# Layer norm of the next block, one row tile per chunk of a gated unit, in place of half a tile per chunk

## The chip, the cores and the metric

The kernel runs on one core of one Trainium2 chip. The metric is the device time of one execution in microseconds (us). Times before are the median of nine executions; one execution was also taken by the hardware profiler, and all durations and positions below come from that one.

The engines go by their short names: PE is TensorE (PEld its weight loads), DVE VectorE, ACT ScalarE, POOL GpSimd, SP the sync engine, which here only issues DMAs.

## The reference

```python
x = A_x                                   # 1 x 2048 x 640, bf16
xn = (x - mean(x)) / sqrt(var(x) + 1e-5)  # layer norm over the last axis

# A: attention, 32 heads of 192, over the last 512 of 2048 cached keys, no mask
q = (xn @ wq) per head                    # wq: 640 x 6144
p = softmax(q @ k.T * 192 ** -0.5)
s = (p @ v, heads side by side) @ wo      # wo: 6144 x 640

# B: gated unit, then a down projection
h = sigmoid(xn @ w_gate) * (xn @ w_up)    # 640 x 1536 each
g = silu(h @ w_down)                      # 1536 x 640
out = x + s * g
```

## The kernel before

The 2048 rows are 16 row tiles of 128 rows (`t`), four of them (`TQ`) to a block of 512 rows (`b`, `NB` = 4). The kernel first makes the normalized rows, transposed (`xnT`), and from them part B (`gate`), block by block, until about 177 us. The rest of the time is attention, eight groups of four heads over four blocks. The order of the instructions on each engine is written out by hand: the scheduler is in manual mode, so each engine runs its instructions in the order in which the program text issues them, and only semaphores and buffers make them wait.

**Gated unit.** `gated(b, f, ...)` (L219) makes one chunk of 128 of the 1536 columns for one block: five matmuls with `wg_sb` and five with `wu_sb` into the two halves of a PSUM bank pair (L227), the sigmoid on ACT (`sig`, L230), then an optional call `between()`, then the product on DVE (`hT`, L233). There are twelve chunks (`NF`) to a block. Four bank pairs take turns (`k`), so that chunk f + 4 needs the bank that the product of chunk f has read. What `between()` issues on DVE stands ahead of that product in DVE's order.

**Down projection.** `down(b, q, k)` (L236) makes `gate` for one row tile: 24 matmuls (L239), a sigmoid (L242), a product (L243).

**Layer norm of a row tile.** It has these parts:
- `stats_half(t, 0)` and `stats_half(t, 1)`: one `bn_stats` on DVE each, of half a row (`st`, L185)
- `stats_end(t)`: `bn_aggr` on DVE (`mv`, L190), then variance plus eps on DVE (`rstd`, L196), and its power of -0.5 on POOL (`rstd`, L197)
- `normal(t)`: subtract and multiply on DVE (`xn`, L203); it waits for POOL
- `turn_dma(t)`: one transposing DMA on SP's queue, from `xn` into `xnT` (L218). Matmuls of that block wait for its landing.

Block 0 has a path of its own at the start. The tiles of blocks 1, 2 and 3 are normalized during the gated unit of the block ahead: `norm_piece(b, i)` (L245) returns the i-th of eight half steps of block b, and the main loop hands it to `gated` as `between`. An even i is the statistics of a tile, an odd i its normalization and transpose. For block 1 they stand in chunks 4 to 11 of block 0, for blocks 2 and 3 in chunks 2 to 9 of the block ahead:

```python
gated(0, f, 0, TB, k, norm_piece(1, f - 4))          # f = 4 to 11
...
gated(b, f, 0, TB, k, norm_piece(b + 1, f - 2) if b + 1 < NB and f < 10 else None)
```

The order around it is: chunks 4 to 11 of block 0; then for b = 1, 2, 3: chunks 0 and 1 of block b, the four down projections of block b - 1, chunks 2 to 11 of block b. So the first matmul of a block's chunk 0 follows the last of chunk 11 of the block ahead, and needs the last row tile of its own block to be transposed.

Other work that the steps touch:
- `load_x(3 * TQ, TQ)` (L149): the rows of block 3, one DMA of 640 KB on SP's queue, behind the transposes of block 1. It takes the buffer that block 1's rows leave.
- `load_group(0)` (L97 to L112): after block 2's last chunk in the text, the first attention group's loads on POOL's queue (query weights `wq_sb` of 960 KB, keys `k_st` of 768 KB, four loads of values `vbuf` of 192 KB) and four copies of keys on POOL (`k_perm`). On POOL they follow directly on the power of row tile 15.
- `turn_keys(0)` (L128): transposing DMAs of the keys on SP, after block 3's last chunk in the text.

Of the kernel before, what the change touches and what calls it, by code (L numbers as in the profile page):

```python
# [15 lines left out]
def kernel(  # L16
# [28 lines left out]
    TB = 512  # L45
    NB = S // TB
    TQ = TB // P
# [45 lines left out]
    def load_group(g):  # L93

        d = grp.setdefault(g, {})
        d["wq"] = load2.tile([P, NCD, GW], BF16, name="wq_sb")
        nc.gpsimd.dma_start(d["wq"][:], wq_r[:, :, g * GW:(g + 1) * GW])  # L97
        kst = load1.tile([P, 4, KC, DH], BF16, name="k_st")
        kv = slice(Sk - W, Sk)
        nc.gpsimd.dma_start(  # L100
            kst[:].rearrange("p h j d -> p h (j d)"),
            A_k_cache[0, 4 * g:4 * g + 4, kv, :].rearrange("h (p j) d -> p h (j d)", j=KC),
        )
        d["v"] = vbuf[g % 2]
        for h in range(4):
            nc.gpsimd.dma_start(  # L106
                d["v"][:, h, :, 0:DH],
                A_v_cache[0, 4 * g + h, kv, :].rearrange("(p j) d -> p j d", j=KC),
            )
        kp = load1.tile([P, 2, KC, DJ, P], BF16, name="k_perm")  # L110
        for h in range(4):
            nc.gpsimd.tensor_copy(  # L112
                kp[:, h // 2, :, :, (h % 2) * H2:(h % 2) * H2 + H2],
                kst[:, h, :, :].rearrange("p c (i j) -> p c j i", j=DJ),
            )
        d["kp"] = kp
# [6 lines left out]
    def turn_keys(g):  # L123
        d = grp[g]
        d["kT"] = load2.tile([P, 2, DJ, W], BF16, name="kT")
        for pr in range(2):
            for c in range(KC):
                nc.sync.dma_start_transpose(  # L128
                    d["kT"][:, pr, :, c * P:(c + 1) * P],
                    d["kp"][:, pr, c, :, :].rearrange("p j i -> p (j i)"),  # L130
                )


    with ExitStack() as bctx:
# [11 lines left out]
        def load_x(t, n):  # L146

            x = xpool.tile([P, n, D], BF16, name=f"x_sb{n}", bufs=1 if n == 2 else 2)
            nc.sync.dma_start(x[:], xf[t * P:(t + n) * P, :].rearrange("(q p) d -> p q d", p=P))  # L149
            for i in range(n):  # L150
                xt[t + i] = x[:, i, :]
# [30 lines left out]
        def stats_half(t, i):  # L182
            if i == 0:
                ln[t] = bwork.tile([P, 2, nc.vector.BN_STATS_DIM], F32, name="st")
            nc.vector.bn_stats(ln[t][:, i, :], xt[t][:, i * (D // 2):(i + 1) * (D // 2)])  # L185

        def stats_end(t):
            mv = bwork.tile([P, nc.vector.BN_AGGR_DIM], F32, name="mv")
            rstd = bwork.tile([P, 1], F32, name="rstd")
            nc.vector.bn_aggr(mv[:], ln[t][:])  # L190
            if t == 0:
                nc.scalar.activation(rstd[:], mv[:, 1:2], AF.Sqrt, bias=eps_t[:], scale=1.0)
                nc.scalar.activation(junk[:], eps_t[:], AF.Sigmoid)
                nc.vector.reciprocal(rstd[:], rstd[:])
            else:
                nc.vector.tensor_scalar(rstd[:], mv[:, 1:2], eps, None, op0=ALU.add)  # L196
                nc.gpsimd.tensor_tensor(rstd[:], rstd[:], mhalf[:], ALU.pow)  # L197
            ln[t] = mv, rstd

        def normal(t):  # L200
            mv, rstd = ln[t]
            xn = xpool.tile([P, D], BF16, name="xn")
            nc.vector.tensor_scalar(xn[:], xt[t], mv[:, 0:1], rstd[:, 0:1],  # L203
                                    op0=ALU.subtract, op1=ALU.mult)
            ln[t] = xn
# [10 lines left out]
        def turn_dma(t):  # L216
            q = t % TQ
            nc.sync.dma_start_transpose(xnT[:, t // TQ, :, q * P:(q + 1) * P], ln[t][:])  # L218
# [3 lines left out]
        def gated(b, f, r0, r1, k, between=None):  # L222
            if b not in hT:
                hT[b] = hpool.tile([P, NF, TB], BF16, name="hT")
            for half, w in ((0, wg_sb), (1, wu_sb)):
                for c in range(NCD):
                    nc.tensor.matmul(bank[k][:, half, 0:r1 - r0], lhsT=w[:, c, f * P:(f + 1) * P],  # L227
                                     rhs=xnT[:, b, c, r0:r1], start=(c == 0), stop=(c == NCD - 1))
            sig = bwork.tile([P, TB], BF16, name="sig")
            nc.scalar.activation(sig[:, 0:r1 - r0], bank[k][:, 0, 0:r1 - r0], AF.Sigmoid)  # L230
            if between is not None:
                between()
            nc.vector.tensor_tensor(hT[b][:, f, r0:r1], bank[k][:, 1, 0:r1 - r0],  # L233
                                    sig[:, 0:r1 - r0], ALU.mult)

        def down(b, q, k):  # L236
            for f in range(NF):
                for d0, d1 in ((0, 512), (512, D)):
                    nc.tensor.matmul(wide(k)[:, d0:d1], lhsT=hT[b][:, f, q * P:(q + 1) * P],  # L239
                                     rhs=wd_sb[:, f, d0:d1], start=(f == 0), stop=(f == NF - 1))  # L240
            sg = bwork.tile([P, D], F32, name="sg", bufs=2)
            nc.scalar.activation(sg[:], wide(k)[:, 0:D], AF.Sigmoid)  # L242
            nc.vector.tensor_tensor(gate[:, b * TQ + q, :], wide(k)[:, 0:D], sg[:], ALU.mult)  # L243

        def norm_piece(b, i):  # L245

            t = b * TQ + i // 2

            def first():
                stats_half(t, 0)  # L250
                stats_half(t, 1)
                stats_end(t)

            def second():
                normal(t)
                turn_dma(t)

            return second if i % 2 else first


        dummy(19)
# [9 lines left out]
        k = 0  # L271
# [28 lines left out]
        k = 3  # L300
        for f in range(4, NF):
            gated(0, f, 0, TB, k, norm_piece(1, f - 4))
            k = (k + 1) % 4
        for b in range(1, NB):
            for f in range(2):
                gated(b, f, 0, TB, k)
                k = (k + 1) % 4
            for q in range(TQ):
                down(b - 1, q, k)
                k = (k + 1) % 4  # L310
            if b == 1:
                load_x(3 * TQ, TQ)
            for f in range(2, NF):
                gated(b, f, 0, TB, k, norm_piece(b + 1, f - 2) if b + 1 < NB and f < 10 else None)
                k = (k + 1) % 4
            if b == 2:
                load_group(0)
            if b == 3:
                turn_keys(0)
        for q in range(TQ):  # L320
            down(NB - 1, q, k)
            k = (k + 1) % 4
# [12 lines left out]
        for m in range(DJ):  # L335
# [3 lines left out]
            k = (k + 1) % 4  # L339
# [114 lines left out]
    for u in range(NU):  # L454
        g, b = u // NB, u % NB
# [67 lines left out]
```

The softmax here doesn't subtract the row's maximum and nothing guards it: scores larger than these inputs give would overflow.

## Time and profile before

| | |
|---|---|
| median of nine executions | 947.35 us (946.27 to 949.1) |
| the profiled execution, its own time | 946.27 us |
| its span in the profile | 944.5 us |
| PE busy | 919.6 us, 97% of the span |
| DVE busy | 471.0 us, 50% |
| ACT busy | 305.8 us, 32% |
| POOL busy | 132.6 us, 14% |
| mean granted PE clock | 0.995 of full |
| blocks 0 to 3 of part B, on the axis | to about 177 us |

The table's shares are over the whole span, and most of it is attention, which the change does not touch. A busy share says how long an engine had an instruction, not whether another waited for it. The chain that ended last is the view that follows, from the last instruction back, who released whom; the waits list how long an engine stood and which instruction released it, where the name given is the one that came last by the profile. The timeline shows instructions in order, each with the idle time ahead of it. All positions are in us from the span's start.

### The profile page before, as it was taken

The numbers are of one execution on the slowest core, as the hardware profiler recorded it, in microseconds if no ns is written. First come the engines' busy times: TensorE is split into PE (matmuls) and PEld (weight loads), VectorE is DVE, ScalarE is ACT, GpSimd is POOL, SyncE is SP. The second block draws the span as 40 slices with busy tenths as digits, with TensorE's granted clock in tenths as the row PEclk, the third lists the DMA queues.
The fourth block names the chain that finished last, engine by engine and source line by source line (L and its number), as shares of the span: only waits on it lengthen the run. The fifth ranks groups of instructions, "written<-read, shape, count | busy, mean of one in ns | idle before, by whom it ended". The sixth has DMA issues, their size and how long they took to land.

```text
span 944.5 us, 18100 instructions
## 1 busy us (share of the span) xinstructions
PE 919.6 (97%) x7962; PEld 546.7 (58%) x8042; DVE 471.0 (50%) x754; ACT 305.8 (32%) x342; POOL 132.6 (14%) x161
## 2 busy tenths in 40 slices
PE   7999979999999999999999999999999999999996
PEld 6455434566666666666666666666666666666664
DVE  5443513345555555555555555555555555555657
ACT  4222212253333333333333333333333333333340
POOL 1000210210020002000200020002000205555000
PEclk9999989999999999999999999999999999999999
DMA  9300240433523253425342433273325334422223
GB/s 312 79 15 15 61 109 1 142 86 49 129 68 76 49 129 67 76 47 130 68 73 52 130 68 76 47 131 68 76 46 131 69 68 80 86 62 62 63 62 90
DMA packets 156767, 76.69 MB, mean 81 GB/s; under 512 B 139024, under 2 KB 150032, under 8 KB 156688
## 3 DMA queue, kind: packets, MB, share of 16 engines
q1 hardware_dynamic: 146288, 42.86, 22.9%
q0 software_dynamic: 7936, 30.94, 11.9%
q10 hardware_dynamic: 2464, 1.74, 0.7%
q8 instruction: 63, 1.03, 0.5%
q14 instruction: 16, 0.13, 0.0%
HBM read 39.45 MB, written 2.62 MB: 45 GB/s over the span
## 4 chain that ended last, share of the span: by engine, by line
PE 95%; DMA 2%; DVE 2%; issue 1%; ACT 0%; SPq 0%; POOL 0%; DVEq 0%
PE bank L381 21%; PE bank L423 21%; PE bank L398 18%; PE bank L363 18%; PE bank L227 10%; PE bank L239 5%; DMA xnT<-xn 1%; PE bank L331 1%; DMA oT<-o_st 0%; DVE st L185 0%; DMA x_sb<-in_A_x_dram 0%; DVE row L445 0%; DVE row L429 0%; DVE o_sb L428 0%; DVE hT L233 0%
## 5 line engine op out<-in xcount | busy, mean ns | idle before, releaser
L367 ACT ACTIVATE E<-bank 128x1024 bf16<-128x1024 f32 x256 | 257.9, 1023 | 477.5 <-PE bank L363 465.6
L381 PE MATMUL bank<-xnT,wq_sb 64*128 64x512 bf16 x1860 | 231.3, 376 | 0.0
L423 PE MATMUL bank<-wo_sb,oT 128*128 128x512 bf16 (+1 forms) x1461 | 224.0, 296 | 5.3 <-DMA oT<-o_st 1.9
L363 PE MATMUL bank<-qT,kT 64*128 64x512 bf16 x1536 | 202.1, 376 | 0.2 <-DVE o_st L404 0.2
L398 PE MATMUL bank<-vbuf,E 128*128 128x193 bf16 x2048 | 191.0, 247 | 0.0
L398 PEld LDWEIGHTS <-E 128*128 128x128 bf16 x2048 | 167.8, 98 | 24.2 <-issue 13.6
L388 DVE CAST qT<-bank 128x1024 bf16<-128x1024 f32 x93 | 113.9, 1225 | 132.8 <-PE bank L381 132.8
L423 PEld LDWEIGHTS <-oT 128*128 128x128 bf16 x1524 | 120.3, 98 | 78.3 <-DMA oT<-o_st 2.6
L381 PEld LDWEIGHTS <-wq_sb 64*128 64x128 bf16 x1860 | 97.0, 100 | 104.8
L363 PEld LDWEIGHTS <-kT 64*128 64x128 bf16 x1536 | 73.1, 94 | 90.2 <-issue 8.9
L404 DVE TENSOR_TENSOR o_st<-bank,rden 128x768 bf16<-128x768 f32 x128 | 122.6, 957 | 4.6 <-DVE rden L403 0.2
L434 DVE TENSOR_TENSOR acc<-bank,acc 128x640 f32<-128x640 f32 x96 | 79.2, 825 | 43.7 <-PE bank L423 43.7
L227 PE MATMUL bank<-xnT,wg_sb 128*128 128x512 bf16 (+1 forms) x296 | 62.4, 340 | 9.9 <-DMA xnT<-xn 5.3
L233 DVE TENSOR_TENSOR hT<-bank,sig 128x512 bf16<-128x512 f32 (+1 forms) x60 | 35.0, 584 | 57.6 <-ACT sig L230 57.5
L227 PE MATMUL bank<-xnT,wu_sb 128*128 128x512 bf16 (+1 forms) x295 | 62.2, 339 | 0.3
L386 DVE COPY seen<-bank 128x2 f32<-128x2 f32 x93 | 14.8, 159 | 94.1 <-PE bank L381 94.0
L403 DVE RECIPROCAL rden<-bank 128x4 f32<-128x4 f32 x128 | 23.3, 182 | 71.3 <-PE bank L398 71.2
L230 ACT ACTIVATE sig<-bank 128x512 bf16<-128x512 f32 (+1 forms) x60 | 30.7, 512 | 85.3 <-PE bank L227 85.3
L239 PE MATMUL bank<-wd_sb,hT 128*128 128x128 bf16 (+1 forms) x376 | 52.4, 297 | 0.4
L106 POOL DMA_DIRECT2D vbuf<-in_A_v_cache_dram x32 | 23.9, 747 | 183.7 <-PE bank L398 183.7
L227 PEld LDWEIGHTS <-wg_sb 128*128 128x128 bf16 x300 | 26.7, 98 | 36.6 <-issue 12.2
L239 PEld LDWEIGHTS <-hT 128*128 128x128 bf16 x384 | 29.7, 98 | 23.1
(49 smaller groups left out, 263.2 us busy)
## 6 DMA issues: line engine op xcount, KB each, us to landing
wq_sb<-in_A_wq_dram POOLq DMA_DIRECT2D x8, 960.0 KB, 6.6
wo_sb<-in_A_wo_dram POOLq DMA_DIRECT2D x8, 960.0 KB, 7.1
k_st<-in_A_k_cache_dram POOLq DMA_DIRECT2D x8, 768.0 KB, 8.4
vbuf<-in_A_v_cache_dram POOLq DMA_DIRECT2D x32, 192.0 KB, 3.0
row<-in_A_x_dram POOLq DMA_DIRECT2D x16, 160.0 KB, 2.5
oT<-o_st SPq DMA_TRANSPOSE x132, 2.6
x_sb<-in_A_x_dram SPq DMA_DIRECT2D x3, 640.0 KB, 11.0
wd_sb<-in_B_w_down_dram SPq DMA_DIRECT2D x1, 1920.0 KB, 14.1
```

The source lines that it names most:

```text
L227: nc.tensor.matmul(bank[k][:, half, 0:r1 - r0], lhsT=w[:, c, f * P:(f + 1) * P], rhs=xnT[:, b, c, r0:r1], start=(c == 0), stop=(c == NCD - 1))
L230: nc.scalar.activation(sig[:, 0:r1 - r0], bank[k][:, 0, 0:r1 - r0], AF.Sigmoid)
L233: nc.vector.tensor_tensor(hT[b][:, f, r0:r1], bank[k][:, 1, 0:r1 - r0], sig[:, 0:r1 - r0], ALU.mult)
L239: nc.tensor.matmul(wide(k)[:, d0:d1], lhsT=hT[b][:, f, q * P:(q + 1) * P], rhs=wd_sb[:, f, d0:d1], start=(f == 0), stop=(f == NF - 1))
L363: nc.tensor.matmul(bank[k][:, i, :], lhsT=kT[r, pr, j, c * P:(c + 1) * P], rhs=q[r, pr * DJ + j, :], start=(j == 0), stop=(j == DJ - 1))
L367: nc.scalar.activation(E[u, pr][:, c, :, :], bank[k][:], AF.Exp, scale=scale_qk)
L381: nc.tensor.matmul(bank[k][:, half, :], lhsT=wq[r, c, col:col + DJ * (P - 1) + 1:DJ], rhs=xnT[r, b, c, :], start=(c == 0 and not second), ...
L388: nc.vector.tensor_copy(qT[u][:, 2 * m:2 * m + 2, :], bank[k][:])
L398: nc.tensor.matmul(o4[:, q, 0:DH + 1], lhsT=e[:, c, h % 2, q * P:(q + 1) * P], rhs=v[:, h, c, 0:DH + 1], start=(c == 0), stop=(c == KC - 1))
L404: nc.vector.tensor_tensor(o_st[u][:, :, h * DH:(h + 1) * DH], o4[:, :, 0:DH], rden[:].to_broadcast([P, TQ, DH]), ALU.mult)
L423: nc.tensor.matmul(wide(k)[:, d0:d1], lhsT=oT[u][:, cc, q * P:(q + 1) * P], rhs=wo[:, cc, d0:d1], start=(cc == 0), stop=(cc == GC - 1))
L434: nc.vector.tensor_tensor(acc[:, t, :], wide(k)[:, 0:D], acc[:, t, :], ALU.add)
```

## The change

`norm_piece` now makes five steps of a block in place of eight. Step i normalizes and transposes tile i - 1, if there is one, and then takes the statistics of tile i, if i is below four. The steps stand in chunks 4 to 8 of the block ahead, for every block. The same instructions are issued; their order changes on DVE alone. On POOL and SP they are issued in the same order, from other chunks.

```diff
         def norm_piece(b, i):
 
-            t = b * TQ + i // 2
-
-            def first():
-                stats_half(t, 0)
-                stats_half(t, 1)
-                stats_end(t)
-
-            def second():
-                normal(t)
-                turn_dma(t)
-
-            return second if i % 2 else first
+            t = b * TQ + i
+
+            def step():
+                if i > 0:
+                    normal(t - 1)
+                    turn_dma(t - 1)
+                if i < TQ:
+                    stats_half(t, 0)
+                    stats_half(t, 1)
+                    stats_end(t)
+
+            return step if i <= TQ else None
...
             for f in range(2, NF):
-                gated(b, f, 0, TB, k, norm_piece(b + 1, f - 2) if b + 1 < NB and f < 10 else None)
+                gated(b, f, 0, TB, k, norm_piece(b + 1, f - 4) if b + 1 < NB and f >= 4 else None)
                 k = (k + 1) % 4
```

The call for block 1, `norm_piece(1, f - 4)`, is the same text; with five steps it now has work in chunks 4 to 8 of block 0.

## The prediction

> **What bounds the kernel now.** I read the page's chain that ended last, then the waits of the first 160 us (only there does the change move anything), then the timeline and the chain around the two longest waits.
>
> ```profile
> PE 95%; DMA 2%; DVE 2%; issue 1%; ACT 0%; SPq 0%; POOL 0%; DVEq 0%
> ...
> PE bank L227 <- DMA xnT<-xn: 5.3, 1, 5.3
> PE bank L227 <- DVE hT L233: 2.2, 1, 2.2
> ```
>
> TensorE sets the end. Vector work counts only where it lets PE stand. From 20 us on, the gated unit does so twice: 2.2 us and 5.3 us. Where are they?
>
> ```profile
> 36.33 1.24 PE L227 MATMUL bank<-xnT,wu_sb 128*128 128x512 bf16 x5
> 36.69 0.44 DVE L203 TENSOR_SCALAR xn<-x_sb,mv,rstd 128x640 bf16<-128x640 bf16 x1
> ...
> 37.16 1.20 SPq L218 DMA_TRANSPOSE xnT<-xn  x1
> ...
> 39.82 1.24 PE L227 MATMUL bank<-xnT,wg_sb 128*128 128x512 bf16 x5 [2.25 <-DVE hT L233]
> ```
>
> This is the step from block 0 to block 1. The last row tile's normalization (tile 7) ends at 37.13, its transposing DMA is issued at 37.16, and the median landing of these is 2.6 us: 39.76, just ahead of the restart at 39.82. The release named, hT, is not the cause: the bank wanted (four take turns) is that of chunk 8, whose product was over by 32.5. So **wait one is tile 7's transpose**. A chunk is 2.155 us (matmul starts 25.54, 27.70, 29.86 in the timeline); chunk 11 began at 35.25, so the next was due at 37.41: 2.41 us lost.
>
> ```profile
> 112.66 0.45 DVE xn L203
> 113.11 0.02 issue
> 113.12 9.77 DMA xnT<-xn
> 122.90 0.25 issue
> 123.14 4.93 PE bank L227 x14
> ...
> q0 software_dynamic: 70, 0.31, 85.3%
> q1 hardware_dynamic: 80, 0.02, 9.1%
> ```
>
> The chain from block 2 to 3: the same transpose (tile 15) takes 9.77 us instead of 2.6. The last two lines are the DMA traffic of 117 to 118 us: while it moves on q1, POOL's loads of attention group 0 fill q0 (weights issued at 112.51, directly after the power of tile 15). Due at 117.70, PE restarts at 123.14: 5.44 us. Then it is slow:
>
> ```profile
> 118.00:120.00 2.00, 0.00 (x0) 0.00 (x0) 0.69 (x1) 0.50 (x1) 0.00 (x0) 0.97 1.10 263
> 122.00:124.00 2.00, 0.86 (x3) 0.33 (x4) 0.00 (x0) 0.00 (x0) 0.00 (x0) 0.50 0.97 253
> 126.00:130.00 4.00, 4.00 (x20) 1.81 (x19) 0.69 (x1) 1.19 (x2) 1.31 (x2) 0.91 0.35 69
> ```
>
> The number before the DMA share (third from the right) is the granted clock: 0.50 until about 126.7. The chunk after this one starts at 127.05, not 123.14 + 2.155 = 125.30, so another 1.75 us.
>
> **What the Trainium skill says.** "TensorE: Matmul & The Clock Gate", Part 1, puts the half clock down to a free-running window of 3413 ns without enough work. The trace agrees: it is low from 119.9 to 126.7, two windows. "DMA: Bandwidth & Descriptors", Queues, rings and completion order, has each engine take turns between queue rows, packet by packet; the 2.6 against 9.8 us fit. The first page also calls DVE strictly first in, first out (Architectural detail), so a normalization waiting for POOL holds the products behind it; the trace order agrees.
>
> **The change, part by part.** No instruction is added or removed; PE, ACT, POOL and SP keep their order, and DVE's changes.
>
> *DVE step.* The durations:
>
> ```profile
> 25.29 0.69 DVE L233 TENSOR_TENSOR hT<-bank,sig 128x512 bf16<-128x512 f32 x1 [1.11 <-ACT sig L230]
> 25.90 0.88 DVE L185 BATCH_NORM_STATS2 st<-x_sb 128x6 f32<-128x320 bf16 x2
> 26.81 0.21 DVE L190 BATCH_NORM_AGGREGATE mv<-st 128x2 f32<-128x12 f32 x1
> 27.05 0.15 DVE L196 TENSOR_SCALAR rstd<-mv 128x1 f32<-128x1 f32 x1
> ...
> 98.94 0.15 DVE L196 TENSOR_SCALAR rstd<-mv 128x1 f32<-128x1 f32 x1
> ...
> 99.83 0.45 DVE L203 TENSOR_SCALAR xn<-x_sb,mv,rstd 128x640 bf16<-128x640 bf16 x1
> ```
>
> From a normalization's start: stats at +0.46 (its 0.44 and a 0.02 gap), aggregate 0.91 later, rstd 0.24 later (so +1.61), then the product and, once POOL's power is done, the next normalization 0.89 after rstd (98.94 to 99.83, the one place where DVE had no pause). A full step is 2.50 us against a chunk of 2.155: DVE falls behind by 0.35 in each of three full steps.
>
> *Block 0.* Tile 4 is as before, normalized at 23.74; then 26.24, 28.74, 31.24 for tiles 5 to 7. Tile 7 ends at 31.68, is issued at 31.70, lands at 34.3 (2.6), 3.1 us ahead of the 37.41 at which it is due. **Wait one goes whole: -2.41.** Its cover is those 3.1 us; even tile 4's 3.6 us landing, beside the first loads, would do. Next late after it: nothing; the queues are empty of the first loads from 28 us on, so the down weights are there.
>
> *Block 1.* No wait before (tile 11 issued at 74.2, due near 80), none after: 0.
>
> *Block 2.* The steps begin two chunks later (f = 4, not 2), end one earlier. Product 3 at 101.26, stats 12 at 101.87 (before, tile 13's), normalization 12 at 104.03 behind product 4. One term differs here: stats 13 begin at 104.49, rstd at 105.64, normalization 13 at 106.53; then +2.50 twice: 109.03 and 111.53. Tile 15's rstd is at 110.64; the power starts 0.30 later and takes 0.55, so POOL issues the group's loads at 111.50 instead of 112.51, and the transpose goes out at 111.99 instead of 113.12. Not a chunk is gained but **1.13 us**, for DVE's lateness takes 1.0 of 2.155. The loads, queued directly behind the power, come 1.01 earlier as well, so the collision stays. I take the same 9.77 us: landing 121.76, restart 122.0, wait 4.30. **-1.13.** Bounds: nothing gained if the transposes are served less kindly, a whole chunk (2.155) if the loads leave it more room. The clock: 4.3 us without a matmul exceeds a window, so it still drops; I leave the 1.75 as it is, 0.8 either way for the phase.
>
> *What else moves.* SP: the x load of tiles 12 to 15 (640 KB, issued at 38.45) stands behind tile 7's transpose and moves up 5.5 us; its rows are read at 97 us, and being behind on the same queue it can't delay that transpose: 0. POOL: six load issues and four key copies 1.0 earlier, wanted after 184 us: 0. The products of chunks 5 to 8 up to 0.8 late: their banks are reused four chunks (8.6 us) after their own start, about 5 us after the product's usual end: 0, and 0.8 is its cover's test.
>
> Sum: -2.41 - 1.13 = -3.54. The profiled execution took 946.27 (span 944.5 and 1.77 around it), so 942.73; the median of nine is 1.08 above it, so 947.35 - 3.54 = **943.8**. In the slower of the nine the 2.2 us gap may have fallen into one window and cost half clock too (up to 1.7 us); that would go as well and is kept for the low end.
>
> **The rivals.** *Only wait one goes.* The late transposes land when the loads let them (q1 moved 80 packets in a microsecond of contention, 330 in the next, as q0 paused); without that pause the landing keeps its time. For it: the loads move with it. Against: they too come 1 us earlier. 944.9.
>
> *Wait two shrinks more.* A whole chunk gives 942.8. If tile 15 passed ahead of the loads (2.6 us, landing 114.6), wait and half clock go: -2.41 - 5.44 - 1.75, 937.8. Against it: it is issued 0.49 after the loads' first issue, before 0.61, hardly different.
>
> *Wait one stays.* If hT really released it, only wait two moves: 946.2. For it, the row's name; against, the fit of 37.16 + 2.6.
>
> *Slower: DVE becomes the bound.* Place: chunks 9 to 11 and the next block's first, which wait for the banks of products 5 to 8. It holds PE once DVE is more than 5 us behind after three full steps, a step of 2.155 + 5/3 = 3.8 us instead of 2.50; each 0.1 beyond costs 0.3 a block, 0.9 in all, and the gain is eaten at 4.2. At 5 us it is 3 x (3 x 2.845 - 5) = 10.6, so 954.4. It needs an unseen stall in each step, such as POOL's 0.55 us power at 2 us or more. Nothing shows one.
>
> **How the numbers follow.** Main case 0.68 (its own range 943.0 to 944.6); only wait one 0.12, a quarter of it inside 0.2%; more at wait two 0.10; wait one stays 0.07; DVE the bound 0.03. A measurement here tells 0.2% (1.9 us) from no change. Faster 0.68 + 0.09 + 0.10 = 0.87; same 0.03 + 0.07 = 0.10; slower 0.03. Low end: a whole chunk at wait two and 1.1 of half clock, 943.8 - 1.0 - 1.1 = 941.7, and 0.3 for scatter; high end: wait one alone and half a microsecond more of half clock, 945.4. Full escape and the last two cases lie outside.
>
> **What would show it.** Right: no PE wait near 37 us; normalizations 2.5 us apart; tile 7 issued near 31.7; a wait of about 4.3 us near 115 (the axis is 2.4 earlier there), half clock behind it; the transpose of tile 15 again 9 to 10 us. Wrong: PE waiting for hT in chunks 9 to 11; a first wait still there; a landing of tile 15 under 5 or over 12 us.

## The result, and the profile after

The changed kernel takes 941.72 us (median of 10; 939.83 to 943.6), the kernel before 947.67 us (now 31 executions): 5.95 us less, a ratio of 0.9938 with a 95% interval from 0.993 to 0.9946. The profiled execution took 942.58 us with a span of 940.8, so against the one of before (946.27) it is only 3.69 us less. Both figures have to be explained: the part that the two profiles agree on, and the 2.3 us by which the medians differ more.

The waits of PE in the stretch of the gated unit (20 to 160 us), after:

```profile
PE bank L227 <- DMA xnT<-xn: 3.6, 1, 3.6
```

One line is left of the two. The wait of 2.2 us at the step from block 0 to block 1 is gone, the one ahead of block 3 is 3.6 us instead of 5.3. DVE's timeline after, in block 0, with one row of POOL's (start, duration, line, operation):

```profile
28.37 0.45 DVE L203 TENSOR_SCALAR xn<-x_sb,mv,rstd 128x640 bf16<-128x640 bf16 x1
28.73 0.88 DVE L185 BATCH_NORM_STATS2 st<-x_sb 128x6 f32<-128x320 bf16 x2
29.64 0.21 DVE L190 BATCH_NORM_AGGREGATE mv<-st 128x2 f32<-128x12 f32 x1
29.89 0.15 DVE L196 TENSOR_SCALAR rstd<-mv 128x1 f32<-128x1 f32 x1
29.96 0.68 DVE L233 TENSOR_TENSOR hT<-bank,sig 128x512 bf16<-128x512 f32 x1
30.18 0.55 POOL L197 TENSOR_TENSOR rstd<-rstd,mhalf 128x1 f32<-128x1 f32 x1 [1.85 <-DVE rstd L196]
30.77 0.45 DVE L203 TENSOR_SCALAR xn<-x_sb,mv,rstd 128x640 bf16<-128x640 bf16 x1
31.59 0.69 DVE L233 TENSOR_TENSOR hT<-bank,sig 128x512 bf16<-128x512 f32 x1 [0.38 <-ACT sig L230]
```

Between the two normalizations lie 2.40 us: the full step, longer than a chunk (2.155). DVE is all but full in it; its longest pause, 0.13 us, is ahead of the second normalization, which starts 0.04 us behind the end of POOL's power. So what sets the step is the chain of statistics, POOL's power and normalization, and the product fits beside it. The last row stands where DVE has caught up: it waits for the sigmoid again. Tile 7's normalization ends at 31.22, so its transpose has some 6 us until block 1 is due at 37.2. The chain of the changed kernel at the step from block 2 to 3, and the stretches around it (granted clock third from the right):

```profile
109.11 9.55 DMA xnT<-xn
118.66 0.25 issue
118.91 7.18 PE bank L227 x20
```

```profile
116.00:118.00 2.00, 0.00 (x0) 0.00 (x0) 0.64 (x1) 0.00 (x0) 0.17 (x1) 0.90 1.06 313
118.00:120.00 2.00, 1.09 (x3) 0.43 (x4) 0.00 (x0) 0.00 (x0) 2.00 (x3) 0.50 0.84 217
...
122.00:124.00 2.00, 2.00 (x7) 0.61 (x5) 0.00 (x1) 0.60 (x1) 0.00 (x0) 0.50 0.50 96
124.00:126.00 2.00, 2.00 (x10) 0.90 (x9) 0.69 (x1) 0.00 (x0) 0.00 (x0) 0.90 0.27 51
```

Tile 15's transpose is slow as before (9.55 us against 9.77), but is issued 6.00 us ahead of its need (109.11 against 115.11) instead of 4.58. From due time to restart PE loses 3.80 us instead of 5.44. Behind that the clock is at half for two windows, and this time it costs 2.70 us, not 1.75: twenty matmuls take 7.01 us up to the down projection instead of 4.31. Before, PE stood through nearly all of the first of the two half-clock windows (119.9 to 123.3, restart at 123.14); now it works at half speed for 2.1 us of the first and for all of the second. That is why this pair of profiles shows less than the medians.

### The profile page after: what moved, and what is told of

Its sections match the earlier page's. It is cut to its first block, busy times and chain, and to the rows that moved or that the text cites. A ratio compares the mean times of both kernels' runs of the same rounds, so it can differ in the third digit from the quotient of the medians.

```text
span 940.8 us, 18100 instructions
## 1 busy us (share of the span) xinstructions
PE 921.0 (98%) x7962; PEld 547.1 (58%) x8042; DVE 471.0 (50%) x754; ACT 305.8 (33%) x342; POOL 132.5 (14%) x161
## 4 chain that ended last, share of the span: by engine, by line
PE 95%; DMA 2%; DVE 2%; issue 1%; ACT 0%; SPq 0%; POOL 0%; DVEq 0%
PE bank L381 21%; PE bank L423 21%; PE bank L398 18%; PE bank L363 18%; PE bank L227 10%; PE bank L239 5%; DMA xnT<-xn 1%; PE bank L331 1%; DMA oT<-o_st 0%; DVE st L185 0%; DMA x_sb<-in_A_x_dram 0%; DVE row L445 0%; DVE row L429 0%; DVE o_sb L428 0%; DVE xnT L214 0%
```

## The experiments

The theory: two separate waits, each of them the last tile's issue plus its landing against the due time, and behind a wait a half clock whose price depends on where the wait falls in a window. The main rival for the surplus: something behind block 3. For the second wait: a transpose slow by itself, or bound to the end of the loads.

### Each half of the change alone

For the first kernel the five steps (here `tile_step`, the text of the changed `norm_piece`) serve block 1 only, for the second blocks 2 and 3 only:

```diff
-            gated(0, f, 0, TB, k, norm_piece(1, f - 4))
+            gated(0, f, 0, TB, k, tile_step(1, f - 4))
```

```diff
-                gated(b, f, 0, TB, k, norm_piece(b + 1, f - 2) if b + 1 < NB and f < 10 else None)
+                gated(b, f, 0, TB, k, tile_step(b + 1, f - 4) if b + 1 < NB and f >= 4 else None)
```

> Five steps for block 1 alone (chunks 4 to 8 of block 0); blocks 2 and 3 keep the eight half steps. Theory one, two separate waits and a half-clock penalty that depends on where the gap falls: PE's wait at the step from block 0 to 1 goes (2.41 us), the one before block 3 stays at 5.4 us; the profile has no PE wait near 37 us. If the median's surplus over the profiles (5.95 against 3.69) comes from half clock behind the first gap, the median falls by 3.5 to 4.5; if it comes from the second gap, by 2.4 only. Rival, the surplus comes from somewhere behind block 3: the median falls by 2.4 and the part behind block 3 is unchanged.

> Five steps for blocks 2 and 3 alone; block 1 keeps its eight half steps. Theory one: the first wait stays (2.25 us), the second shrinks from 5.44 to 3.8, so 1.6 in the waits. If half clock at the second gap makes the surplus, the median falls by 3.5 or more; if it is the first gap's, by 1.6. The two kernels' gains should add up to the 5.95 of the whole change.

Block 1 alone: 944.22 us, ratio 0.9962 (0.9949 to 0.9974) to before, 3.6 us. Blocks 2 and 3 alone: 945.83 us, ratio 0.998 (0.9972 to 0.9988), 1.9 us. Together 5.5 of the 5.95. PE's waits, first of the one, then of the other kernel:

```profile
PE bank L227 <- DMA xnT<-xn: 4.9, 1, 4.9
```

```profile
PE bank L227 <- DMA xnT<-xn: 3.4, 1, 3.4
PE bank L227 <- DVE hT L233: 2.2, 1, 2.2
```

Each half acts on its own wait and leaves the other's: the first removes it, the second shortens it. The first saves more than its 2.41 us, though its interval (2.5 to 4.8 us) barely leaves that out; the second little over its 1.6. That points to the first wait for the surplus, but does not settle it: in the profile of the first kernel the second wait, still 5.0 us, happens to cost 1.67 us of half clock, less than in any profile of the kernel before, so a part of its saving can be chance.

### The loads kept behind the transpose

One POOL copy, put in ahead of the loads, reads a column that tile 15's transpose writes; POOL is in order, so the loads follow the landing. Added to the kernel before and to the changed one:

```diff
+    guard = const.tile([P, 1], BF16, name="guard")
...
             if b == 2:
+                nc.gpsimd.tensor_copy(guard[:], xnT[:, 3, 0, TB - 1:TB])
                 load_group(0)
```

> The kernel before, with one POOL copy of a single column of block 3's transposed rows (last row tile) ahead of the first attention group's loads: POOL can issue them only when tile 15's transpose has landed. Theory one (the transpose is late because it shares the DMA engines with those loads): it lands in 2.6 us instead of 9.8, at 115.7 against 117.7 due, so the second wait and its half clock go: 5.44 + 1.75 = 7.2 less, 940.5. What is left is the first gap alone, so the times should lie in two groups up to 1.7 us apart if that gap costs half clock in some executions. Rival (the transpose is slow by itself): no change, 947.7.

> The changed kernel with the same POOL copy ahead of the loads. Theory one: tile 15's transpose lands in 2.6 us, 3 us ahead of its need; no PE wait is left in part B, no half clock, and the times lie within about 0.5 us of each other: 941.72 less 3.8 of wait and some 1.7 to 2.7 of half clock, 935.5 to 936.5. Rival (the transpose is slow by itself): 941.7.

Measured 939.71 us (939.09 to 940.7) and 936.83 us (936.68 to 937.73), ratios 0.9916 (0.9903 to 0.993) and 0.9885 (0.9872 to 0.9899). I had expected 940.5, and 935.5 to 936.5: the first came out 0.8 lower, the second 0.3 higher. The first kernel's five times (939.09 to 940.7) are too few to show the two groups that I expected. PE's waits with the copy in the kernel before (line numbers one up) with its restart at block 1, and POOL's timeline with it in the changed kernel:

```profile
PE bank L228 <- DVE hT L234: 2.0, 1, 2.0
...
40.69 1.24 PE L228 MATMUL bank<-xnT,wg_sb 128*128 128x512 bf16 x5 [2.04 <-DVE hT L234]
```

```profile
108.29 0.55 POOL L198 TENSOR_TENSOR rstd<-rstd,mhalf 128x1 f32<-128x1 f32 x1 [1.85 <-DVE rstd L197]
...
111.78 0.19 POOL L318 COPY guard<-xnT 128x1 bf16<-128x1 bf16 x1 [2.94 <-DMA xnT<-xn]
111.90 1.06 POOL L98 DMA_DIRECT2D wq_sb<-in_A_wq_dram  x1
```

POOL waits 2.94 us and starts the loads some 3 us later; the transpose lands in 2.4 us, and the changed kernel has no PE wait left in part B. So the transpose is not slow by itself: the loads make it so, and they can wait. With the second wait gone from both, the kernels differ by 2.88 us. In their two profiles (2.84 us apart) the first wait makes 2.20 of it, with full clock behind it; the start is 1.0 us longer in the kernel before, by a half-clock window from 9.56 to 12.97 that the change does not touch, and the rest takes 0.4 back. So this pair shows the first wait itself, and no half clock of its own. The changed kernel with the copy is among the fastest measured; two kernels below (937.08 and 936.64 us) are not told apart from it.

### The same steps two chunks earlier

For blocks 2 and 3; those of block 1 stay.

```diff
-                gated(b, f, 0, TB, k, norm_piece(b + 1, f - 4) if b + 1 < NB and f >= 4 else None)
+                gated(b, f, 0, TB, k, norm_piece(b + 1, f - 2) if b + 1 < NB else None)
```

> The changed kernel with the five steps of blocks 2 and 3 in chunks 2 to 6 instead of 4 to 8 (block 1's stay). The loads still follow tile 15's power directly, so the collision stays and the transpose should again take 9 to 10 us. Theory one (the second wait is issue time plus that landing, against the due time): the issue moves up by 4.2 us, the wait of 3.8 goes with some half a microsecond to spare, the half clock with it: 936.5 to 937.5, as with the POOL copy. Rival (the end of the loads' traffic is what ends the wait, and it is put off by more than it moves): part of the wait stays, 938 to 941.

Measured 937.08 us (936.74 to 938.35), ratio 0.9889 (0.9873 to 0.9906). Landings of the four transposes of block 3, and the chain around the step to block 3:

```profile
DMA to landing us min/median/max: 2.6/2.6/9.3
```

```profile
99.86 20.07 PE bank L227 x93
```

The slowest landing is still 9.3 us, but the chain is matmuls without a break: an earlier issue hides what it does not cure. The loads moved with it, from 108.60 to 104.75, so the run alone does not exclude that the transpose waits for their end. The landings do: here it lands at 114.55 and the last of the loads at 116.79; in the changed kernel at 118.66 and 120.74, in the kernel before at 122.89 and 126.50.

### More executions of both kernels

The same kernels, profiled again, to see what differs between executions.

> The kernel before once more, for a second profile. The first one had full clock behind the first gap and in the start, and a time near the lowest of all. Theory (a clock window that runs free of the kernel): in about half of the executions the first gap of 2.25 us is followed by one window at half clock, 1.7 us; the start, up to chunk 4 of block 0, differs by up to 1.2 us for the same reason. Expected 945.8 to 949.1, with those places slower where the time is higher. Rival: the scatter of before lies behind 180 us.

> The same again: a third profile of the kernel before, 945.8 to 949.1; half clock behind the first gap where the time is over 947.

> A fourth profile of the kernel before: 945.8 to 949.1; second wait 5.0 to 5.5 us, 1.7 to 3 us lost to half clock behind it; behind the first wait half clock only if its 2.4 us fall into one window, which in the three so far (at most 1.9 us in one) they did not.

> A second profile of the changed kernel. Theory: the waits are as in the first (3.6 to 3.8 us ahead of block 3, none ahead of block 1); the half clock behind the second wait costs between 1.7 and 2.7 us by the phase of the window, the start up to 1.2. Expected 939.8 to 943.6, the sum of these two terms moving with the time.

> A third profile of the changed kernel: 939.8 to 943.6; wait ahead of block 3 of 3.4 to 3.8 us, half clock behind it for one or two windows of 3.41 us (1.7 to 2.7 us lost), or none if the wait is split evenly over two windows.

They took 947.63, 946.63 and 948.19 us (before), 941.83 and 940.15 us (after). The fourth profile of before shows what the first could not. Its PE timeline at the step from block 0 to 1, and the stretches:

```profile
36.61 1.24 PE L227 MATMUL bank<-xnT,wu_sb 128*128 128x512 bf16 x5
40.10 1.78 PE L227 MATMUL bank<-xnT,wg_sb 128*128 128x512 bf16 x5 [2.25 <-DVE hT L233]
41.67 2.34 PE L227 MATMUL bank<-xnT,wu_sb 128*128 128x512 bf16 x5
43.80 1.38 PE L227 MATMUL bank<-xnT,wg_sb 128*128 128x512 bf16 x5
```

```profile
40.00:42.00 2.00, 1.90 (x6) 0.77 (x7) 0.00 (x0) 0.00 (x0) 0.00 (x0) 0.67 0.79 177
42.00:44.00 2.00, 2.00 (x6) 0.76 (x5) 0.00 (x0) 0.00 (x0) 0.00 (x0) 0.50 0.40 147
```

The wait of 2.25 us is followed by half clock: the five matmuls of a half chunk take 2.34 us instead of 1.24. The third profile of the changed kernel shows the opposite at the second wait. Its waits, and the stretches there:

```profile
PE bank L227 <- DMA xnT<-xn: 3.5, 1, 3.5
```

```profile
116.00:118.00 2.00, 0.00 (x0) 0.00 (x0) 0.69 (x1) 0.09 (x1) 0.00 (x0) 1.00 1.04 309
118.00:120.00 2.00, 1.09 (x6) 0.53 (x7) 0.00 (x0) 0.00 (x0) 0.85 (x2) 1.00 0.88 225
```

A wait of nearly the same size, and full clock throughout. Read off the profiles in this way, in us (first column: its first recorded matmul; at 20.36 and 20.19 the first of five is missing in the trace, so that these start some 0.2 us earlier; losses at half clock: time from the restart to the down projection, less 4.31):

| | start of chunk 4 | first wait | half clock | second wait | half clock | sum of the last four |
|---|---|---|---|---|---|---|
| before, 946.27 | 20.36 | 2.41 | 0 | 5.44 | 1.75 | 9.60 |
| before, 947.63 | 21.40 | 2.41 | 0 | 5.07 | 2.56 | 10.04 |
| before, 946.63 | 20.48 | 2.41 | 0 | 5.15 | 2.09 | 9.65 |
| before, 948.19 | 20.42 | 2.41 | 1.69 | 5.02 | 2.33 | 11.45 |
| after, 942.58 | 20.19 | 0 | 0 | 3.80 | 2.70 | 6.50 |
| after, 941.83 | 20.25 | 0 | 0 | 3.46 | 1.69 | 5.15 |
| after, 940.15 | 20.15 | 0 | 0 | 3.61 | 0 | 3.61 |

The means are 10.19 and 5.09, 5.1 us apart: 2.41 for the first wait and 0.42 for its half clock, 1.55 for the second and 0.72 for its half clock. With 0.47 of the start, which the change does not touch and where the samples differ by chance, that is 5.6, and the mean times of these executions (947.18 and 941.52) are 5.66 apart. The last matmul of part B's down projections says the same without the sum: it starts at 177.86 on average before and at 172.27 after, 5.59 us earlier, and from there to the end of the span it is 767.4 to 767.7 us before and 767.2 to 767.6 after. So the difference lies ahead of 180 us, and the rival "behind block 3" falls. How often half clock follows the first wait is open: one in four here, one in six with the profiles of the kernel before with the copy and of blocks 2 and 3 alone, where I had written half; and 947.63 had none there though over 947, its excess being in the start, where it has a half-clock window. So the shares of half clock are those of these seven executions; for the medians' 5.95 us they say where the surplus can lie, and not how large each share is.

### How late DVE may be

To size the rival in which DVE becomes the bound, the changed kernel with the POOL copy was given extra `bn_stats` of a constant tile in each block's last step, between the normalization and the product of chunk 8: nine, and eighteen.

```diff
+                if i == TQ:
+                    for _ in range(18):
+                        nc.vector.bn_stats(spare[:], warm[:, 0:320])
```

> The changed kernel with the POOL copy ahead of the loads (no PE wait in part B) and, in the last step of each block, nine extra bn_stats of a constant tile on DVE (0.44 us each, 3.96 us) between tile 3's normalization and the product of chunk 8. Theory (a product has 5 us of cover, since its bank is wanted only four chunks after its own start): the products from chunk 8 on are up to 3.8 us late, PE does not wait, 936.8 within 0.5. Rival (DVE lateness costs PE directly): 3.8 in each of three blocks, up to 11 us more.

> The same with eighteen extra bn_stats (7.9 us) in the last step of each block. Theory: the product of chunk 8 comes 7.8 us late, 2.8 us beyond its cover of 5; PE waits about 2.8 us for that bank at chunk 0 of the next block, once in each of three blocks, 8.4 us, with half clock behind some of these waits: 945 to 950. If the cover is larger than 5 us, less. A wait in the profile should name the product (L233's line, two further down in this file).

Nine: 936.64 us (936.62 to 937.46), the same as without them, and no PE wait. Eighteen: 954.48 us (953.14 to 954.69). PE's waits of the latter, then DVE and PE in its timeline:

```profile
PE bank L229 <- DVE hT L235: 11.5, 3, 3.9
```

```profile
32.17 9.48 DVE L257 BATCH_NORM_STATS2 spare<-warm 128x6 f32<-128x320 bf16 x18
41.57 2.47 DVE L235 TENSOR_TENSOR hT<-bank,sig 128x512 bf16<-128x512 f32 x4
...
42.30 1.77 PE L229 MATMUL bank<-xnT,wg_sb 128*128 128x512 bf16 x5 [3.85 <-DVE hT L235]
```

The eighteen took 9.48 us, 0.53 each, not 0.44. The product of chunk 8 would have begun at about 32.64 (normalization's end at 32.26 plus the 0.38 of the changed kernel's profile), so it is 8.9 us late; PE, due at 38.29, restarts at 42.30, 4.0 later. The cover is 8.9 - 4.0 = 4.9 us. Three such waits are 12.0, the clock is at half for one window behind each (1.7 each), and 936.8 + 12.0 + 5.1 = 953.9 (the profiled execution, at 954.69, has one such window more in the start). The forecast of 945 to 950 missed by the stats' length and by a half clock behind all three.

## Why the prediction was right or wrong

The direction and both places were right; the median was 2.1 us below the predicted 943.8, inside the range near its low end. It saved 2.4 us more than the 3.54 of the sum (the median of before is 0.3 higher over 31 executions than over nine). Of this, the means of the table put 0.4 into the second wait, 1.1 into half clock, and 0.5 into the start, which is chance and no merit of the change; the remaining 0.4 no profile shows.

- **Wait one goes whole.** Right: 2.41 in each profile before, 0 after. The landing of tile 7 was the cause, not hT as the row's name had it: in the profile before it lands at 39.73 and PE restarts at 39.82. In the kernel before with the copy the transpose took 0.2 us less, landed at 40.60, and PE restarted at 40.69: the wait follows the landing (2.20 instead of 2.41).
- **The full step is longer than a chunk.** Right in kind, 2.40 instead of 2.50. The mis-sized term is the stats' start, 0.36 after the normalization's instead of 0.46: the next instruction starts before the recorded end of the one ahead. The prediction's own lines had a case: the product at 25.29 takes 0.69, and the stats behind it start at 25.90. Over the three full steps that makes the issue 0.3 earlier than worked out (1.42 us gained instead of 1.13).
- **The same landing of 9.77.** Right in the main: 9.2 to 9.6 in the three profiles after, 9.3 to 9.8 before. With the earlier issue (1.42) and a landing 0.22 shorter the second wait shrank by 1.64 in the first pair of profiles, and by 1.55 on average, for the predicted 1.13.
- **"I leave the 1.75 as it is".** The step that was wrong, though held in the range. Two things were missing from the sum: the first wait's half clock, named but kept for the low end, belongs in the median with its share (0.42 in four profiles); and the shorter second wait cost less half clock in these profiles (mean 1.46 at 3.6 us against 2.18 at 5.2). The second is not established: the single values, 0 to 2.70 and 1.75 to 2.56, overlap. I said that 4.3 us exceeds a window, so the clock still drops; 3.6 us exceeds one too, and in one of three it did not.
- **Covers.** The products' cover was put at about 5 us and measured 4.9; DVE was late by half a microsecond (the product at 29.96, its sigmoid's end at 29.46), for the 0.8 worked out. The rival with DVE as the bound is real but far off: three blocks would have to lose 5.95 us, so by estimate 2.0 each beyond the cover, 6.9 us of lateness against 0.5.
- **Escape ahead of the loads** was put at 937.8; by the POOL copy it gives 936.83, by earlier steps 937.08.

## What to carry to other kernels

Work that hides behind PE has a due time: find the last of it and count its distance to the need from issue to landing, before anything else about its size. A transpose that some consumer will wait for should go out ahead of bulk loads, or the loads be held until it has landed; here one tiny copy did that, worth 4.9 us on top of the change. Here a PE gap of 2.4 to 5.4 us cost its length and, by chance, 0 to 2.7 us of half clock, so forecast the median with the chance of that in it, and take several profiles before matching a sum to a difference.

## What was not expected of the hardware

The clock's window can be read off the profiles, from the granted clock in short stretches. In the kernel with block 1's steps alone the half clock begins at 8.45 us in the start and again at 121.09; in the second profile of before at 9.76 and 122.40; both 112.64 apart, 33 times 3.413. In the fourth, 40.66 and 122.58 are 24 times that apart. The Trainium skill ("TensorE: Matmul & The Clock Gate", Part 1) gives a free-running window of 3413 ns, and this agrees; but its advice to avoid gaps over about 3 us (Why this matters for your kernels) is too mild here. A gap of 2.41 us cost 1.69.

What counts is the share of one window, counted in steps of 3.413 us from such a drop. 1.84 us without a matmul in a window (before, 37.98 to 39.82) did not drop the clock; 2.04 us (before, 117.86 to 119.90) and 2.07 us (after, second profile, 116.78 to 118.85) did. In the third profile of the changed kernel a window ends inside the second wait, at 117.10 (240 windows ahead of the drop at 936.30, when the matmuls are over): the wait falls apart into 1.65 and 1.81 us, and the clock stays full. From these figures I estimate that 2.25 us without a matmul, as in the first wait, drops the clock in about half of its positions against the window; one of six seen does not contradict that. And a window with matmuls for 2.1 of its 3.41 us (after, first profile, 118.91 to 121.0) did not bring full clock back, one with 3.2 us (blocks 2 and 3 alone, 122.42 to 125.63) did.
